# First and last chunk of 128 rows instead of 256, and weight preparation without its clamp, in a fused top-k attention and channel mix

## The chip, the core and the metric

The kernel runs on one core of a Trainium2 chip. The metric is the time on the device, in microseconds (us); it is 1204.24 us before the change (median of three runs, 1203.76 to 1204.57). A TensorE matmul clock of 1.00 in the profile means 2.4 GHz; the lower of its two levels is 1.2 GHz.

## What is computed

```python
# attention, batch 8, 8 heads, 576 rows, head size 64, top 32 of each row
scores = q @ k.T / 8
kth = 32nd largest score of the row
scores = where(scores >= kth, scores, -1e9)
attn = exp(scores - max); attn = attn / (sum(attn) + 1e-9)
x = heads side by side of (attn @ v)          # 8 x 576 x 512
# channel mix
x_prev = x moved down by one row
xk = mu_k * x + (1 - mu_k) * x_prev
xr = mu_r * x + (1 - mu_r) * x_prev
out = sigmoid(xr @ w_r) * (relu(xk @ w_k) ** 2 @ w_v)   # w_k 512x1024, w_v 1024x512, w_r 512x512
```

q, k and v are float32. The mix weights are float64; they reach the kernel as pairs of 32-bit words, and the kernel makes two fp32r halves of each (hi and lo).

## The kernel before

**Slots.** pipeline() writes one instruction order by hand. Attention has 288 tiles of 128 rows (64 rows of each head of a pair, or two heads' rows together). In slot n tile n is scored (L207, L211) and kept (L216), tile n-1 gets its candidates (L240), tile n-2 its best values (L243, L246), tile n-3 is counted (L254, L257), tile n-4 gets its threshold, exponential and mask (L833, L262, L265, L268), tile n-5 is transposed (L280, L283), a finished unit is weighed with v (L330) in slot n-6, and placed in xT (L342) in slot n-7. ORDER (L43) gives the order of steps within a slot, on each engine's queue.

**Passes.** A batch is walked in passes (PARTS, L31). A pass takes some rows for all four head pairs, and a pair has one or two units of 1, 2 or 4 tiles each. The keys of up to four pairs stay loaded, so only the first pass of a batch loads them. load_keys, load_queries and load_v put DMAs on SyncE's queue in slots that loads() works out from the start of each pair.

**Mix chunks.** The mix runs in chunks of 256 consecutive rows over all batches (SIZES, L29; 18 of them). have() (L653) says whether a chunk's rows are placed, and it says no while the weights are not done. Then begin() queues xd, xm on GpSimd (L355, L360, L365), finish() the two halves xh (ScalarE, L380) and xl (GpSimd, L381). The matmul work is cut into pieces: gate pieces (pz, 3 matmuls of 512 columns, 8 pieces in a chunk), hidden pieces (ph, 6 matmuls of as many columns as the chunk has rows, 16 pieces), value pieces (pv, 3 matmuls of 512 columns, 16 pieces). All go through three() (L385 to L387): hi x hi, hi x lo, lo x hi. The generator mix_steps orders them: gates of chunk c, second half of the values of chunk c-1, hidden pieces of c, first half of the values of c, gates of c+1. relu, square and lo half of the hidden values follow on ScalarE and GpSimd (L402 to L406), tanh of the gate on ScalarE (L418).

**The planner.** Lanes keeps a credit for each engine. TensorE's grows by 3.90 a slot up to 4.45; scores take 0.92 of it, the transpose 0.47, a weighed unit of four tiles 2.7, a mix piece 0.71 (0.56 in the last 36 slots), whatever its width. A piece goes out while at least 0.74 of its cost is there, at most four in a slot. Soft tasks on ScalarE and GpSimd go out by their own lanes' credit; the steps of the weights are charged to no lane.

**Weights.** weight_steps yields 20 blocks of 128 x 512, one a slot from slot 0 (four of w_r, eight of w_k, eight of w_v). In the slot after its DMA a block's high words go through Abs on ScalarE (L151) and a clamp on GpSimd (L152), then three bit steps on VectorE (L156 to L158). One slot later: the coarse half on GpSimd (L126), the low words on ScalarE (L162), a product on GpSimd (L163) and the remainder on TensorE (L130, L132). Another slot later ScalarE writes the lo half (L135). The PSUM tiles of this, wbits and wlo, share the two buffers of psM with pz, ph and pv. The stage buffers lie in hh and hl, which the mix uses later for its hidden values.

Of the kernel before, what the change touches and what calls it, by code (L numbers as in the profile page):

```python
# [9 lines left out]
F32 = mybir.dt.float32  # L10
# [17 lines left out]
CH = 256  # L28
SIZES = [CH] * (B * S // CH)  # L29
WHOLE = [(0, 4), (256, 4), (512, 1)]  # L30
PARTS = [[(0, 4)], [(256, 4)], [(512, 1)]], [[(0, 1), (64, 2)], [(192, 4)], [(448, 2)]], \  # L31
    [[(0, 2)], [(128, 4)], [(384, 2), (512, 1)]], [[(0, 1)], [(64, 4)], [(320, 4)]]
SCALE = 1.0 / math.sqrt(D)
# [3 lines left out]
TINY = 1e-30  # L37
ZERO = 2.0 ** -15
NEG = -3.0e38
PACE, TENSOR, SHARE, PIECE, CAP, MOST = 4.60, 3.90, 0.74, 0.71, 4.45, 4  # L40
END, HASTE = 36, 0.56
EXPS, EVAC = 4, (0, 'et')
# [4 lines left out]
def topk_attention_channel_mix(ctx: ExitStack, tc: tile.TileContext, q, k, v, mu_k, mu_r, w_k, w_v, w_r, out):  # L47
    nc = tc.nc
# [46 lines left out]

    def load_mu():
        for i, m in enumerate((mu_k, mu_r)):
            nc.sync.dma_start(mu[:, i, :], m.rearrange("(h p) -> p h", p=128))
        nc.vector.tensor_scalar(nmu, mu, -1.0, 1.0, op0=OP.mult, op1=OP.add)

# [18 lines left out]
    def weight_block(g, L, n, block, hi, lo, half):  # L119
# [30 lines left out]
        def magnitude():  # L150
            nc.scalar.activation(mag.bitcast(F32), high.bitcast(F32), AF.Abs)  # L151
            nc.gpsimd.tensor_scalar(mag.bitcast(F32), mag.bitcast(F32), ZERO, 1.0, op0=OP.max, op1=OP.mult)  # L152

# [276 lines left out]
    def mix_steps(g, chunks, L):  # L430
# [43 lines left out]

        def hiddens(c, x):
            c.hh = g.one.tile([128, NFB, CH], F32R, name="hh")
            c.hl = g.one.tile([128, NFB, CH], F32R, name="hl")
            c.written = {}
            for f in range(0, NFB, 2):
                X = Env()  # L480
                for part in range(4):
                    while len(g.ready) < (2 + f // 4) * HP:
                        yield 1
                    while part == 3 and len(g.hiddens) > 1 and not g.hiddens[-2].done:
                        yield 1
                    yield 0
                    hidden(g, f, part, *x, c.hh, c.hl, c.n, X, L)
                c.written[f // 2] = X.done
                g.hiddens.append(X.done)
# [125 lines left out]
    def pipeline(g):  # L615
# [30 lines left out]
        def chunks():  # L646
            t0 = 0
            for size in SIZES:
# [4 lines left out]
                def have(i, C=C, t0=t0, size=size):  # L653
                    if "weights" in state or min(state["heads"][2 * i:2 * i + 2]) < t0 + size:
                        return False
# [9 lines left out]
                t0 += size  # L665

        steps, state["weights"] = mix_steps(g, chunks(), L), weight_steps(g, L)
        state["next"] = None
# [50 lines left out]
        prep(g, P, P.batch, P.hp, P.c0, P.c1)  # L719
        load_mu()  # L720
        n = 0
        while n < total + 8 or "next" in state or L.busy():
# [5 lines left out]
            def loads():  # L728
                for N, t in coming(n):
                    early = N.n > 1  # L730
                    if N.own and n == max(starts[N.n] - (5 if early else 4), N.free):
                        load_keys(g, N, N.batch, N.hp)
                    if n == max(starts[N.n] - (4 if early else 3), starts[N.n - 2] - 1 if N.n > 2 else 0):
                        load_queries(g, N, N.batch, N.hp, N.c0, N.c1)
                    if n == starts[N.n - 1] + 6:
                        load_v(g, N, N.batch, N.hp)
# [90 lines left out]
            def weights():  # L827
                if "weights" in state and next(state["weights"], 0) == 0:
                    del state["weights"]

            def eighth():
# [69 lines left out]
    with tc.If(again > 0):  # L901
        with tc.For_i(0, B, 1) as b, ExitStack() as stack:
            g = Env()
            open_pools(stack, g, "_again")
            L = Direct()
# [65 lines left out]
```

## Time and profile before

| | before |
|---|---|
| median of three runs | 1204.24 us |
| profiled execution | 1203.7 us, span 1201.9 us |
| busy: TensorE, VectorE, GpSimd, ScalarE | 1117.5, 1065.4, 1024.8, 994.8 us |
| mean granted TensorE clock | 0.963 |

All four engines are at work for most of the span, so the shares of busy time don't say by themselves what a stage waits for. The profile's names: PE is TensorE, PEld its weight loads, DVE VectorE, ACT ScalarE, POOL GpSimd, SP SyncE. L152 is line 152 of the kernel. "<-POOL hl L152" behind an instruction names what ended the idle time before it. Starts of matmuls one after the other are closer than the length of one, since they overlap.

### The profile page before, as it was taken

How to read it: one execution, taken by the hardware profiler on the slowest of the kernel's cores; microseconds unless marked ns; L12 is line 12 of the kernel's file. 1: busy time of each engine (PE TensorE's matmuls, PEld its weight loads, DVE VectorE, ACT ScalarE, POOL GpSimd, SP SyncE). 2: the span in 40 equal slices, each digit the busy share in tenths (PEclk: the TensorE clock that was granted, in tenths of full speed). 3: DMA queues.
4: the chain of work that ended last, by engine and by line, in shares of the span. 5: the costliest groups of instructions: out<-in, count | busy, mean ns of one | idle time of the engine just before them, and what ended most of it. 6: DMA issues, size and time to landing. Idle time of an engine off the chain costs nothing.

```text
span 1201.9 us, 32805 instructions
## 1 busy us (share of the span) xinstructions
PE 1117.5 (93%) x10625; PEld 865.8 (72%) x10625; DVE 1065.4 (89%) x5999; ACT 994.8 (83%) x2121; POOL 1024.8 (85%) x1099
## 2 busy tenths in 40 slices
PE   4787799899999999999999999999999999999987
PEld 1343577686878787878787877787878777877876
DVE  4989999999999999999999999999999999999500
ACT  3777799998899899989898989998989899978611
POOL 5999987888889898989898888898989798988863
PEclk9777799899999999999999999999999999999989
DMA  5343114122332133212221124112421133111000
GB/s 160 110 128 104 28 47 108 50 54 57 85 75 55 50 89 76 57 48 57 67 58 48 43 77 101 49 43 67 101 75 45 49 81 90 46 38 39 29 10 29
DMA packets 161363, 78.77 MB, mean 66 GB/s; under 512 B 125344, under 2 KB 154016, under 8 KB 161184
## 3 DMA queue, kind: packets, MB, share of 16 engines
q1 hardware_dynamic: 161184, 76.59, 23.9%
q8 instruction: 87, 1.43, 0.5%
q14 instruction: 92, 0.75, 0.2%
HBM read 67.11 MB, written 9.44 MB: 64 GB/s over the span
## 4 chain that ended last, share of the span: by engine, by line
PE 53%; ACT 14%; POOL 11%; DVE 9%; issue 2%; ACTq 0%; POOLq 0%; DVEq 0%
PE ps L330 10%; PE ps L207 8%; PE ph L385 4%; ACT sc L216 4%; POOL sg L257 4%; PE pv L385 4%; PE pt L280 4%; PE ph L386 4%; PE ph L387 4%; PE pv L387 3%; PE pv L386 3%; PE pz L385 3%; ACT sg L254 2%; PE pz L387 2%; PE pz L386 2%; DVE cand L240 2%
## 5 line engine op out<-in xcount | busy, mean ns | idle before, releaser
L240 DVE MAX8 cand<-sc 128x8 f32<-128x82 f32 (+1 forms) x2016 | 464.6, 231 | 4.8 <-ACT sc L216 4.5
L257 POOL TENSOR_TENSOR sg<-sc,sg 128x576 f32<-128x576 f32 x288 | 410.6, 1427 | 37.9 <-ACT sg L254 36.3
L216 ACT ACTIVATE sc<-ps 128x576 f32<-128x576 f32 x288 | 187.8, 652 | 96.2 <-PE ps L207 84.8
L254 ACT ACTIVATE sg<-sc,seen 128x576 f32<-128x576 f32 x288 | 225.6, 783 | 21.9 <-DVE seen L833 17.8
L268 DVE SCALAR_TENSOR_TENSOR E<-sc,seen,se 128x576 f32<-128x576 f32 x288 | 232.9, 809 | 0.8 <-PE ps L211 0.3
L265 ACT ACTIVATE se<-sc,seen 128x576 f32<-128x576 f32 x288 | 215.7, 749 | 15.0 <-DVE E L268 14.5
L833 DVE MAX8 seen<-sg 128x8 f32<-128x576 f32 x288 | 215.9, 750 | 5.7 <-POOL sg L257 5.2
L207 PE MATMUL ps<-K,qs 64*128 64x288 f32 x1024 | 202.2, 472 | 14.7 <-ACT sc L216 6.4
L283 ACT ACTIVATE et<-pt 128x640 f32<-128x640 f32 x288 | 204.6, 711 | 6.4 <-PE pt L304 3.4
L330 PE MATMUL ps<-et,v_in 128*64 128x128 f32 (+1 forms) x2560 | 165.4, 273 | 21.1 <-ACT sc L216 18.5
L280 PEld LDWEIGHTS pt<-ident,E 64*128 64x128 f32 x2880 | 134.2, 140 | 64.4 <-ACT sg L254 13.0
L243 DVE MAX8 seen<-cand 128x8 f32<-128x56 f32 x864 | 176.7, 205 | 0.1
L385 PE MATMUL ph<-xh,wk 128*128 128x256 f32 x576 | 172.1, 299 | 0.0
L330 PEld LDWEIGHTS ps<-et,v_in 128*64 128x64 f32 x2560 | 134.6, 141 | 51.1 <-ACT sc L216 36.4
L386 PE MATMUL ph<-xl,wk 128*128 128x256 f32 x576 | 163.1, 283 | 0.0
L387 PE MATMUL ph<-xh,wk 128*128 128x256 f32 x576 | 162.7, 282 | 0.0
L280 PE MATMUL pt<-ident,E 64*128 64x64 f32 x2880 | 141.1, 226 | 4.4 <-DVE E L268 2.4
L207 PEld LDWEIGHTS ps<-K,qs 64*128 64x128 f32 x1024 | 80.4, 191 | 75.2 <-issue 29.1
L381 POOL TENSOR_TENSOR xl<-xm,xh 128x512 fp32r<-128x512 f32 x72 | 91.2, 1287 | 36.8 <-ACT xh L380 36.6
L385 PE MATMUL pv<-wv,hh 128*128 128x512 f32 x288 | 122.1, 424 | 0.0
L387 PE MATMUL pv<-wv,hl 128*128 128x512 f32 x288 | 115.2, 400 | 7.2 <-POOL hl L406 7.1
L246 DVE MATCH_REPLACE8 cand<-seen,cand 128x56 f32<-128x56 f32 x576 | 115.1, 200 | 0.0
(91 smaller groups left out, 2321.7 us busy)
## 6 DMA issues: line engine op xcount, KB each, us to landing
v_in<-in_v SPq DMA_DIRECT2D x192, 128.0 KB, 2.5
qs<-in_q SPq DMA_DIRECT2D x96, 128.0 KB, 2.8
K<-in_k SPq DMA_DIRECT2D x64, 144.0 KB, 2.9
out<-eb SPq DMA_DIRECT2D x36, 256.0 KB, 2.1
vr_in<-in_v SPq DMA_DIRECT2D x96, 32.0 KB, 2.4
hh<-in_moe_w_v SPq DMA_DIRECT2D x6, 512.0 KB, 3.7
qs<-in_q SPq DMA_DIRECT2D x32, 96.0 KB, 2.6
hh<-in_moe_w_k SPq DMA_DIRECT2D x5, 512.0 KB, 3.4
```

The lines of the kernel that those rows point to most:

```text
L207: nc.tensor.matmul(g.ps[:, e], lhsT=P.qs[h, T.j, x:x + 128], rhs=P.K[h, T.j], start=True, stop=True)
L216: nc.scalar.activation(T.sc.rearrange("p (e k) -> p e k", e=2), T.ps, AF.Copy)
L240: nc.vector.max(T.cand[:, 8 * i:8 * i + 8], T.sc[:, CUTS[i]:CUTS[i + 1]])
L254: nc.scalar.activation(T.side, T.sc, AF.Sign, bias=T.top[:, 23:24], scale=-1.0, accum_out=T.cnt)
L257: nc.gpsimd.tensor_mul(T.side, T.sc, T.side)
L268: nc.vector.scalar_tensor_tensor(T.e, T.sc, T.thr, g.pe, op0=OP.is_ge, op1=OP.mult, accum_out=T.rs)
L280: nc.tensor.transpose(g.pt[:, n, c * 64:(c + 1) * 64], T.e[h, k0:k0 + 128], ident[h, h])
L330: nc.tensor.matmul(pa[hs[j]], lhsT=lhsT, rhs=ms[c][j], start=(c == 0), stop=(c == NKC))
L385: nc.tensor.matmul(ps, lhsT=sh, rhs=mh, start=first, stop=False)
L386: nc.tensor.matmul(ps, lhsT=sh, rhs=ml, start=False, stop=False)
L387: nc.tensor.matmul(ps, lhsT=sl, rhs=mh, start=False, stop=last)
L833: nc.vector.max(M.top[:, 24:32], M.side)
```

## The change

The order of PARTS is turned by two, so that batch 0 begins with a pass of 128 rows and the last batch ends with one. SIZES begins and ends with a chunk of 128; all others keep 256 rows, moved by 128. The chunks need not wait for the weights in have() any more; instead hiddens() waits until three slots after the last block. Weight blocks begin in slot 2 (WAIT). The clamp in magnitude() goes; the Abs before it is scaled by 2^-112 instead. `nmu` is made in slot 3's list, and a pair's keys can be due in slot 0.

```diff
--- before.py
+++ after.py
@@ -26,18 +26,19 @@
 HP = H // 2
 NFB = FF // 128
 CH = 256
-SIZES = [CH] * (B * S // CH)
+SIZES = [CH // 2] + [CH] * (B * S // CH - 1) + [CH // 2]
 WHOLE = [(0, 4), (256, 4), (512, 1)]
-PARTS = [[(0, 4)], [(256, 4)], [(512, 1)]], [[(0, 1), (64, 2)], [(192, 4)], [(448, 2)]], \
-    [[(0, 2)], [(128, 4)], [(384, 2), (512, 1)]], [[(0, 1)], [(64, 4)], [(320, 4)]]
+PARTS = [[(0, 2)], [(128, 4)], [(384, 2), (512, 1)]], [[(0, 1)], [(64, 4)], [(320, 4)]], \
+    [[(0, 4)], [(256, 4)], [(512, 1)]], [[(0, 1), (64, 2)], [(192, 4)], [(448, 2)]]
 SCALE = 1.0 / math.sqrt(D)
 NCH = 7
 KEYS = 4
 CUTS = [82 * i for i in range(NCH)] + [S]
 TINY = 1e-30
-ZERO = 2.0 ** -15
+LOWER = 2.0 ** -112
 NEG = -3.0e38
 PACE, TENSOR, SHARE, PIECE, CAP, MOST = 4.60, 3.90, 0.74, 0.71, 4.45, 4
+WAIT = 2
 END, HASTE = 36, 0.56
 EXPS, EVAC = 4, (0, 'et')
 ORDER = """count below exp wpool high wmul norm evac best0 c0 drop0 c1 best1 c2 drop1 first score turn inv loads keep sums sign c3 best2 c4 bounds eighth norm2 et late act c5 early thr c6 mask place mix weigh wpe dve pool weights""".split()
@@ -93,10 +94,10 @@
         g.psT = p("psT", 1, space=PSUM)
         g.psM = p("psM", 2, space=PSUM)
 
-    def load_mu():
+    def load_mu(L):
         for i, m in enumerate((mu_k, mu_r)):
             nc.sync.dma_start(mu[:, i, :], m.rearrange("(h p) -> p h", p=128))
-        nc.vector.tensor_scalar(nmu, mu, -1.0, 1.0, op0=OP.mult, op1=OP.add)
+        L.at(3, "dve", lambda: nc.vector.tensor_scalar(nmu, mu, -1.0, 1.0, op0=OP.mult, op1=OP.add))
 
     def weight_steps(g, L):
 
@@ -148,8 +149,7 @@
         mag, exp = g.mag[n % 2].bitcast(U32), g.exp[n % 2].bitcast(U32)
 
         def magnitude():
-            nc.scalar.activation(mag.bitcast(F32), high.bitcast(F32), AF.Abs)
-            nc.gpsimd.tensor_scalar(mag.bitcast(F32), mag.bitcast(F32), ZERO, 1.0, op0=OP.max, op1=OP.mult)
+            nc.scalar.activation(mag.bitcast(F32), high.bitcast(F32), AF.Abs, scale=LOWER)
 
         def shift():
             bits = g.psM.tile([128, 512], U32, name="wbits", tag="pm")
@@ -473,6 +473,8 @@
                 g.gates.append(G)
 
         def hiddens(c, x):
+            while not g.staged():
+                yield 1
             c.hh = g.one.tile([128, NFB, CH], F32R, name="hh")
             c.hl = g.one.tile([128, NFB, CH], F32R, name="hl")
             c.written = {}
@@ -651,7 +653,7 @@
                 C.n, C.rows, C.pieces = size, out_rows[t0:t0 + size], None
 
                 def have(i, C=C, t0=t0, size=size):
-                    if "weights" in state or min(state["heads"][2 * i:2 * i + 2]) < t0 + size:
+                    if min(state["heads"][2 * i:2 * i + 2]) < t0 + size:
                         return False
                     if C.pieces is None:
                         state["start"] = t0
@@ -664,6 +666,7 @@
                 yield C
                 t0 += size
 
+        g.staged = lambda: n > state.get("made", n) + 2
         steps, state["weights"] = mix_steps(g, chunks(), L), weight_steps(g, L)
         state["next"] = None
 
@@ -717,7 +720,7 @@
         total = len(where)
         P = new_pair(0)
         prep(g, P, P.batch, P.hp, P.c0, P.c1)
-        load_mu()
+        load_mu(L)
         n = 0
         while n < total + 8 or "next" in state or L.busy():
             p = where[n] if n < total else None
@@ -728,7 +731,7 @@
             def loads():
                 for N, t in coming(n):
                     early = N.n > 1
-                    if N.own and n == max(starts[N.n] - (5 if early else 4), N.free):
+                    if N.own and n == max(starts[N.n] - (5 if early else 4), N.free, 0):
                         load_keys(g, N, N.batch, N.hp)
                     if n == max(starts[N.n] - (4 if early else 3), starts[N.n - 2] - 1 if N.n > 2 else 0):
                         load_queries(g, N, N.batch, N.hp, N.c0, N.c1)
@@ -825,8 +828,9 @@
                 work(MOST)
 
             def weights():
-                if "weights" in state and next(state["weights"], 0) == 0:
+                if n >= WAIT and "weights" in state and next(state["weights"], 0) == 0:
                     del state["weights"]
+                    state["made"] = n
 
             def eighth():
                 if M:
@@ -901,6 +905,7 @@
     with tc.If(again > 0):
         with tc.For_i(0, B, 1) as b, ExitStack() as stack:
             g = Env()
+            g.staged = lambda: True
             open_pools(stack, g, "_again")
             L = Direct()
             xT = new_batch(g)
```

## Rows read from the trace of the kernel before

**Rows 1.** Busy time by stage: window and its length, then each engine, granted clock, DMA.
```profile
14.20:133.80 119.60, 89.97 (x506) 48.21 (x508) 105.85 (x474) 86.59 (x166) 112.72 (x92) 0.76 0.35 107
...
300.00:1100.00 800.00, 781.60 (x7902) 623.03 (x7902) 767.81 (x4442) 714.44 (x1544) 706.70 (x778) 1.00 0.25 64
...
1117.30:1144.90 27.60, 27.60 (x259) 23.59 (x256) 11.66 (x51) 15.63 (x32) 20.58 (x22) 1.00 0.03 12
...
1144.90:1193.50 48.60, 45.28 (x238) 38.11 (x236) 2.07 (x3) 10.30 (x18) 26.37 (x26) 0.93 0.05 17
```

**Rows 2.** Chain that ended last, 226 to 231 us: start, length, what.
```profile
226.38 0.82 DVE E L268 x2
...
229.83 0.82 DVE E L268 x2
```

**Rows 3.** L216 on ScalarE, one in each slot: durations ns, first and last start.
```profile
L216 ACT ACTIVATE sc<-ps x288: 627/652/722, 7.2 to 1117.3; 128x576 f32<-128x576 f32 x144
```

**Rows 4.** GpSimd groups, 0 to 140 us: busy us, mean ns, idle before them, releaser.
```profile
L152 POOL TENSOR_SCALAR hl<-hl 128x512 f32<-128x512 f32 x20 | 38.3, 1915 | 12.3 <-ACT hl L151 12.2
...
L257 POOL TENSOR_TENSOR sg<-sc,sg 128x576 f32<-128x576 f32 x21 | 29.6, 1409 | 0.0
...
L163 POOL TENSOR_TENSOR wprod<-wfine,early 128x512 fp32r<-128x512 f32 x20 | 25.3, 1267 | 2.2 <-ACT wfine L162 2.2
...
L126 POOL TENSOR_SCALAR wv<-early 128x512 fp32r<-128x512 f32 x8 | 6.5, 819 | 0.9 <-DVE early L157 0.9
```

**Rows 5.** VectorE groups, 0 to 140 us: the line that waits for the clamp.
```profile
L156 DVE TENSOR_SCALAR wbits<-hl 128x512 uint32<-128x512 uint32 x20 | 13.9, 695 | 15.7 <-POOL hl L152 15.6
```

**Rows 6.** VectorE in order of time: start, length, instruction, idle before it and releaser.
```profile
15.78 0.69 DVE L156 TENSOR_SCALAR wbits<-hl 128x512 uint32<-128x512 uint32 x1 [6.23 <-POOL hl L152]
...
49.06 0.69 DVE L156 TENSOR_SCALAR wbits<-hl 128x512 uint32<-128x512 uint32 x1 [0.23 <-POOL hl L152]
...
54.63 0.69 DVE L156 TENSOR_SCALAR wbits<-hl 128x512 uint32<-128x512 uint32 x1 [0.22 <-POOL hl L152]
...
74.17 0.69 DVE L156 TENSOR_SCALAR wbits<-hl 128x512 uint32<-128x512 uint32 x1 [0.22 <-POOL hl L152]
```

**Rows 7.** ScalarE in order of time, one weight slot.
```profile
75.14 0.65 ACT L162 ACTIVATE wfine<-hh 128x512 f32<-128x512 uint32 x1
```

**Rows 8.** TensorE in order of time: first gate matmuls of chunk 0 and chunk 16.
```profile
149.26 0.50 PE L385 MATMUL pz<-wr,xh 128*128 128x512 f32 x1
...
1114.93 0.40 PE L385 MATMUL pz<-wr,xh 128*128 128x512 f32 x1
```

**Rows 9.** TensorE in order of time, from the last placed tile on.
```profile
1144.50 0.28 PE L386 MATMUL ph<-xl,wk 128*128 128x256 f32 x1
...
1144.62 0.28 PE L387 MATMUL ph<-xh,wk 128*128 128x256 f32 x1
...
1155.64 0.79 PE L387 MATMUL pv<-wv,hl 128*128 128x512 f32 x1 [3.14 <-POOL hl L406]
...
1157.08 0.63 PE L387 MATMUL pv<-wv,hl 128*128 128x512 f32 x1
...
1157.51 0.63 PE L385 MATMUL pz<-wr,xh 128*128 128x512 f32 x1
...
1192.84 0.40 PE L386 MATMUL pv<-wv,hh 128*128 128x512 f32 x1
...
1193.07 0.39 PE L387 MATMUL pv<-wv,hl 128*128 128x512 f32 x1
```

**Rows 10.** GpSimd in order of time: the last placed tile.
```profile
1144.15 0.74 POOL L342 TENSOR_TENSOR xT<-sum,ri 128x256 f32<-128x256 f32 x1 [1.31 <-ACT sum L336]
```

**Rows 11.** Chain that ended last, 152 to 163 us: attention matmuls at full clock.
```profile
152.28 0.69 PE ps L207 x4
...
152.96 0.30 PE pt L280 x10
...
160.09 2.40 PE ps L330 x40
```

## The prediction, written before the changed kernel ran

> **What bounds the kernel now.** I read four views in this order: busy time by stage, the groups of the opening, the queue of one engine there, and the order of instructions in the closing stage. Time goes in slots: slot n scores tile n of the attention, and each slot has one L216, so their starts date it [rows 3]. The stages differ [rows 1]. From 300 to 1100 us TensorE is busy 782 and VectorE 768 of 800 us; both are full, a slot is 3.7 us, and little can be won. Between 14.2 and 133.8 us (slots 2 to 22, with a weight block in each) a slot takes 5.98 us, and there VectorE is busy 106 and GpSimd 113 of 119.6. After the last attention tile TensorE is alone: from the last placed tile (ends at 1144.9, [rows 10]) to the last value matmul at 1193.5 it holds 238 matmuls in 48.6 us [rows 1, 9]. What then follows, 8.4 us of closing steps in the span, is not touched.
>
> In a weight slot GpSimd has four long steps: the mask product 1.41, the clamp 1.92, the coarse half 0.83, the product 1.27, together 5.43 us [rows 4]. The slot's period, from one L156 to the next, is 5.57 us [rows 6]. So the clamp looks worth 1.92 x 20 = 38 us. It isn't: VectorE waits for the clamp only 0.22 us in each of 14 such slots, and its own queue is 5.57 - 0.22 = 5.35 us long. A VectorE slot without weights is 3.45 us [rows 2]; the block's three steps make the other 1.9. VectorE is the next bound, right below the first.
>
> **The change part by part.** The profiled execution took 1203.7 us (span 1201.9), 0.5 below the median of 1204.24; the sum goes against 1203.7.
>
> *The clamp (20 GpSimd instructions out).* ScalarE's scaled Abs is the same instruction as the Abs before, so it costs nothing new. L156 then waits for that Abs, which ends 1.9 us earlier than the clamp. VectorE idled 15.6 us in 18 waits for the clamp [rows 5], 6.2 of it at the first block [rows 6]. The other 9.4 go: -9.4 (0 to -9.4).
>
> *Blocks begin in slot 2.* The same 20 blocks stand two slots later. The 6.2 us wait was for the first block's DMA and clamp; now the tiles of slots 2 and 3 are computed meanwhile. Against that, three head pairs of keys and queries are loaded in the first two slots (pairs have two tiles now), all on SyncE's queue ahead of block 0, and slot 2 waits for its keys. Between 0 and -6.2; I take half, -3.1. The row of `nmu` moves to slot 3, off the start, and is needed only in slot 10: nothing.
>
> *First chunk of 128.* Its eight tiles are placed in slot 14, not 22, and have() no longer waits for the weights. The xm/xh/xl chain takes two slots, so four gate pieces go out together in slot 16, amid the weights, where TensorE and ScalarE are not full. But psM has two buffers, and each weight slot takes two (wlo, wbits). The gates' pz makes three: the L156 of slot 16 must wait until pz is read by tanh (L418), in slot 17 behind exp, fine and wfine. Behind L156 stands all of VectorE's next slot. L156 starts at 74.17 and the wfine of the following slot ends at 75.79 [rows 6, 7], so tanh's half microsecond makes that wait at least 2.1 us; with the 12 gate matmuls ahead of it, 0.23 us each at full clock and 0.43 at 1.2 GHz [rows 9], it is up to 6.3. I take +4.5 (0 to +6.3). The hidden pieces wait for staged() until slot 25. What is queued there is only this generator; by slot 36 it has done 28 pieces, worth 20 full ones, where the kernel before, whose first gate started in slot 26 [rows 8], had done 26; those six are made up, because chunk 1 follows at once where the kernel before still waited for the rows of its second chunk. Chunk c+1 then runs where c ran, eight slots later, and the middle is unchanged (0 +- 2).
>
> *Last chunk of 128.* Before: of the 238 matmuls in the last 48.6 us, 116 are hidden ones at 0.12 us and 120 of 512 columns at 0.23 [rows 9]: 41.7 us. The other 7 are a 3.14 us wait for hl and some 15 matmuls at the half clock right after it, 0.43 apart instead of 0.23 [rows 9]. After: chunk 17 (256 rows) is there eight slots before the last tile. Before, chunk 16's gates began in slot 286, four after the earliest possible one [rows 8]; I expect chunk 17's in slot 291 or 292, done when the last tile is placed (slot 294). Then remain 12 value matmuls of chunk 16, 96 hidden and 48 value of chunk 17, 12 gate, 96 half-width hidden and 24 value of the last one: 96 of 512 columns x 0.23 = 22.1, 96 x 0.12 = 11.5, and the half-width ones. No row shows a 128-column matmul of this type. From 0.233 at 512 and 0.12 at 256 columns the line gives 0.063 at 128; the dear end is the plain f32 product, 128 columns in two instructions, 40 of them in 2.40 us with two side by side [rows 11], so 0.12 for an instruction's turn and 0.24 for a product. I take 0.063, since the two rows are of the same type and on one line through nearly zero: 6.0 us. The sum is 39.6; xl ahead of the gates is half as long, so half the wait and half the slow matmuls stay: 2 to 3 us. 48.6 - 42 = -6.6, rounded to -7. With chunk 17's gates still open it is -1, with chunk 16's values done -10.
>
> Sum: -9.4 - 3.1 + 4.5 - 7 = -15: 1203.7 - 15 = 1189 us.
>
> **The rivals.**
> *A 128-column matmul costs what a 256-column one does* (0.12, bound by its weight load): the last chunk's 96 cost 5.4 us more, the first chunk's are hidden in slots 25 to 31: 1194 us. For it: each has its own weight load. Against it: ten transposes, each with a 128-column load, take 0.30 us [rows 11]. The Trainium skill (TensorE: Matmul & The Clock Gate, section LDWEIGHTS) says a load takes its columns over 1.2 GHz; that would be about 0.107 us each, an estimate by that page, and 4.2 us on the last chunk. The transposes' rows disagree, but they use half the array's rows each.
>
> *It costs what a plain f32 product does* (0.24). This ends slower. Place: the hidden pieces of the first and last chunk, whose only columns are 128 where every hidden one now has 256. Price: the last chunk's 96 cost 96 x 0.177 = 17 us more, all on the path. The first chunk's 96 take 23 us of TensorE in some six slots; attention there takes 0.69 + 0.30 + 0.60 [rows 11] of 3.45, which leaves 11 us, so 12 more. 1189 + 29 = 1218 us. Gain and loss are equal at 0.17 us per matmul. For it: the planner counts a piece as 0.71 whatever its width, so nothing would hold back; the operands are four bytes wide, as f32 ones. Against it: one instruction each, not two.
>
> *VectorE alone rules the opening*: the waits for the clamp turn into waits for keys, ScalarE and pz, the opening gains only 14 x 0.22 = 3 and pays 4.5. Then only the closing is left: 1203.7 + 1.5 - 7 = 1198 us. For it: 5.35 against 5.57. Against it: the long waits are not of that kind.
>
> **How the numbers follow.** Forecast 0.43 (1189, own range 1181 to 1196); same price as 256 columns 0.16 (1194); VectorE alone 0.11 (1198); f32 price 0.30 (1218, 1211 to 1224). No measurement of this kernel tells less than about 0.2%, 2.4 us, from no change. Slower takes the f32 case, 0.30; same 0.06, the upper ends of the two middle cases; faster the other 0.64. The range must take in part of the f32 case: 1179 to 1216.
>
> **What would show it.** The period of L156 in the weight slots falls to about 5.35; 3.7 would mean that VectorE wasn't the bound, 5.57 that GpSimd wasn't. The L156 of slot 16 has one wait of 2 to 6 us released by tanh. The first pz comes in slot 16, the first ph in slot 25. The starts of the 128-column ph matmuls are 0.06 apart; at 0.12 the first rival holds, at 0.2 or above the second, and the forecast is wrong. From the last placed tile to the last value matmul it takes 42 us. If the middle's slots are longer than 3.7 us, my claim that only the ends move is wrong.

## The result: slower by 0.9%, and the loss lies in the middle

The changed kernel takes 1214.91 us (median, 1213.68 to 1215.98), against 1204.00 of the kernel before beside it: a ratio of 1.0094 [1.0078, 1.011]. The forecast was 1189, faster. The time lies just inside the upper end of the range, but that end was there for another reason, which the trace refutes.

| | before | after |
|---|---|---|
| profiled execution, span | 1203.7, 1201.9 us | 1215.4, 1213.4 us |
| busy: TensorE, VectorE, GpSimd, ScalarE | 1117.5, 1065.4, 1024.8, 994.8 us | 1130.1, 1073.9, 989.7, 995.9 us |
| mean granted TensorE clock | 0.963 | 0.973 |

GpSimd lost 35 us of work and the span grew by 11.5. Busy time by stage in the changed kernel (window, its length, each engine, granted clock, DMA), to be read beside [rows 1]: the weight slots 4 to 22, the same 800 us of the middle, the last slots, and the closing stage from the last placed tile on.

```profile
20.90:134.40 113.50, 88.87 (x523) 50.83 (x523) 105.79 (x448) 87.46 (x175) 79.01 (x91) 0.83 0.38 110
300.00:1100.00 800.00, 775.06 (x7756) 615.25 (x7753) 760.57 (x4379) 703.22 (x1514) 693.85 (x752) 0.99 0.24 62
1130.40:1156.60 26.20, 24.29 (x224) 19.52 (x221) 11.86 (x50) 15.79 (x36) 23.67 (x29) 1.00 0.13 34
1156.60:1205.20 48.60, 48.30 (x303) 42.61 (x301) 2.06 (x3) 11.49 (x24) 26.89 (x36) 1.00 0.05 17
```

In the weight slots GpSimd is down to 79 of 113.5 us, so the clamp is gone, and VectorE alone is near full there, at 105.8 us. In the middle both full engines are less busy than before: TensorE 775 for 782, VectorE 761 for 768, with fewer instructions in the same 800 us. Something else holds them up. The closing stage, from the last placed tile to the last value matmul, takes 48.6 us as before, though it now has 303 matmuls and no half clock.

The starts of L216, one in each slot, date the slots. All times of stages and slots here come from one profiled execution of each kernel; executions of one kernel differ by up to 6 us in the whole. Here is how much later than before each kernel starts a slot, in us, the experiments below among them (minus is earlier; before: slot 24 at 139.8, 36 at 186.2, 112 at 462.8, 287 at 1117.3, last value matmul at 1193.07 [rows 9]):

| kernel | 24 | 36 | 112 | 287 | last value matmul |
|---|---|---|---|---|---|
| after | +0.2 | -4.0 | +8.5 | +13.1 | +11.7 |
| before with the moved rows alone | 0.0 | -1.0 | +13.9 | +14.4 | +14.5 |
| after without the moved rows | -5.2 | -5.5 | -5.2 | -5.1 | -5.2 |
| after, hl ahead of xm | +0.1 | -4.1 | +3.5 | +0.9 | -6.0 |
| before, hl ahead of xm | +0.3 | +0.4 | -0.8 | -4.3 | -10.8 |
| after without the moved rows, hl ahead of xm | -5.5 | -6.9 | -3.1 | -4.7 | -12.3 |
| the same, coarse half moved | -13.9 | -14.1 | -11.7 | -13.6 | -21.2 |

The change gains 4.0 us by slot 36, loses 12.5 between slots 36 and 112, another 4.6 up to slot 287, and gets 1.4 back after it. Between slots 24 and 287 it takes 990.4 us where the kernel before took 977.5: +12.9 where I had put 0 +- 2.

What the slots wait for shows in the chain of work that ended last. First the kernel before, then the changed one, slots 48 to 112 (227.9 to 462.8 and 225.8 to 471.3 us): the chain's share of that stretch by line.

```profile
by line: PE ps L330 12.1%; PE ps L207 10.6%; ACT sc L216 6.2%; PE pt L280 5.0%; PE ph L385 4.7%; ACT sg L254 4.6%; PE pv L385 4.1%; ACT et L283 4.1%; PE ph L386 4.0%; PE ph L387 3.9%; ACT se L265 3.8%; PE pv L387 3.4%; PE pv L386 3.4%; PE p
```

```profile
by line: POOL sg L257 10.8%; PE ps L330 9.8%; PE ps L207 9.7%; POOL hl L406 6.6%; ACT sc L216 4.4%; PE pv L387 4.4%; POOL r L405 4.2%; PE pv L385 4.2%; PE ph L385 4.1%; POOL xl L381 4.0%; PE pv L386 3.5%; PE pt L280 3.5%; PE ph L386 3.3%; P
```

Before, no line of GpSimd stands among the first thirteen. Now four do, with a quarter of the stretch: the mask product, the square (r), its lo half (hl), and the lo half of the next chunk's rows (xl). One place of it, on GpSimd of the changed kernel in order of time (start, length, instruction):

```profile
234.85 2.56 POOL L381 TENSOR_TENSOR xl<-xm,xh 128x512 fp32r<-128x512 f32 x2
237.36 1.42 POOL L257 TENSOR_TENSOR sg<-sc,sg 128x576 f32<-128x576 f32 x1
238.74 0.74 POOL L342 TENSOR_TENSOR xT<-sum,ri 128x256 f32<-128x256 f32 x1
239.42 1.05 POOL L405 TENSOR_TENSOR r<-r 128x512 f32<-128x512 f32 x1
240.55 1.27 POOL L406 TENSOR_TENSOR hl<-r,hh 128x512 fp32r<-128x512 f32 x1
```

On TensorE, the value matmul that reads this hl, and the scores that are queued behind it:

```profile
241.87 0.50 PE L387 MATMUL pv<-wv,hl 128*128 128x512 f32 x1 [2.95 <-POOL hl L406]
...
244.38 0.76 PE L207 MATMUL ps<-K,qs 64*128 64x288 f32 x4
```

And on ScalarE the keep that reads the scores, from which the rest of the tile's chain starts:

```profile
245.27 0.65 ACT L216 ACTIVATE sc<-ps 128x576 f32<-128x576 f32 x1 [3.51 <-PE ps L207]
```

The last hl of chunk 1 stands behind both xl of chunk 2 in GpSimd's queue. The scores of the next tile are written behind that value matmul and start only at 244.38 us, so a value matmul without its hl holds them too. This is the place of slot 51, the longest of the middle (6.93 us). The gates of chunks 2 to 5 go out first in slots 51, 67, 83, 99; each of these four slots is longer than 4.5 us (6.93, 4.82, 4.63, 4.61).

### The profile page after: what moved, and what is told of

The parts are those of the page before. It is cut to its first block, busy times and chain, and to the rows that moved or that the text cites. A ratio compares the mean times of both kernels' runs of the same rounds, so it can differ in the third digit from the quotient of the medians.

```text
span 1213.4 us, 33035 instructions
## 1 busy us (share of the span) xinstructions
PE 1130.1 (93%) x10721; PEld 877.6 (72%) x10721; DVE 1073.9 (89%) x5999; ACT 995.9 (82%) x2133; POOL 989.7 (82%) x1098
## 4 chain that ended last, share of the span: by engine, by line
PE 55%; POOL 18%; ACT 12%; DVE 10%; issue 2%; SPq 1%; DMA 0%; DVEq 0%; ACTq 0%; POOLq 0%
PE ps L330 11%; PE ps L207 8%; POOL sg L257 6%; PE ph L385 4%; PE ph L386 4%; PE pv L385 4%; PE ph L387 4%; PE pv L387 4%; ACT sc L216 4%; PE pt L280 4%; PE pv L386 3%; POOL hl L406 3%; PE pz L385 3%; POOL xl L381 2%; POOL r L405 2%
## 5 line engine op out<-in xcount | busy, mean ns | idle before, releaser
L216 ACT ACTIVATE sc<-ps 128x576 f32<-128x576 f32 x288 | 188.1, 653 | 118.8 <-PE ps L207 103.7
L254 ACT ACTIVATE sg<-sc,seen 128x576 f32<-128x576 f32 x288 | 225.8, 784 | 17.0 <-DVE seen L837 16.5
L265 ACT ACTIVATE se<-sc,seen 128x576 f32<-128x576 f32 x288 | 215.9, 750 | 12.0 <-DVE E L268 11.5
L330 PE MATMUL ps<-et,v_in 128*64 128x128 f32 (+1 forms) x2560 | 168.2, 276 | 23.1 <-ACT sc L216 20.4
L385 PE MATMUL ph<-xh,wk 128*128 128x256 f32 (+1 forms) x608 | 179.7, 296 | 0.0
L386 PE MATMUL ph<-xl,wk 128*128 128x256 f32 (+1 forms) x608 | 171.3, 282 | 0.3 <-POOL xl L381 0.3
L387 PE MATMUL ph<-xh,wk 128*128 128x256 f32 (+1 forms) x608 | 170.8, 281 | 0.0
L385 PEld LDWEIGHTS ph<-xh,wk 128*128 128x128 f32 x608 | 117.1, 193 | 4.8
L381 POOL TENSOR_TENSOR xl<-xm,xh 128x512 fp32r<-128x512 f32 (+1 forms) x76 | 91.7, 1229 | 31.1 <-ACT xh L380 30.9
```

Of the source, the lines that this page charges most:

```text
L216: nc.scalar.activation(T.sc.rearrange("p (e k) -> p e k", e=2), T.ps, AF.Copy)
L254: nc.scalar.activation(T.side, T.sc, AF.Sign, bias=T.top[:, 23:24], scale=-1.0, accum_out=T.cnt)
L330: nc.tensor.matmul(pa[hs[j]], lhsT=lhsT, rhs=ms[c][j], start=(c == 0), stop=(c == NKC))
L385: nc.tensor.matmul(ps, lhsT=sh, rhs=mh, start=first, stop=False)
L386: nc.tensor.matmul(ps, lhsT=sh, rhs=ml, start=False, stop=False)
L387: nc.tensor.matmul(ps, lhsT=sl, rhs=mh, start=False, stop=last)
```

## The experiments

Two questions: which half of the change loses the time, and by what. My theory after reading the trace was the order on GpSimd above. The rivals: the weights' half of the change loses it; chunks are taken too early; the moved 128-column matmuls cost it; the first chunk among the weights sets the mix back.

**The moved rows alone.** The kernel before with the new passes and chunks; chunks still wait for the weights and the clamp stays.

```diff
-SIZES = [CH] * (B * S // CH)
+SIZES = [CH // 2] + [CH] * (B * S // CH - 1) + [CH // 2]
-PARTS = [[(0, 4)], [(256, 4)], [(512, 1)]], [[(0, 1), (64, 2)], [(192, 4)], [(448, 2)]], \
-    [[(0, 2)], [(128, 4)], [(384, 2), (512, 1)]], [[(0, 1)], [(64, 4)], [(320, 4)]]
+PARTS = [[(0, 2)], [(128, 4)], [(384, 2), (512, 1)]], [[(0, 1)], [(64, 4)], [(320, 4)]], \
+    [[(0, 4)], [(256, 4)], [(512, 1)]], [[(0, 1), (64, 2)], [(192, 4)], [(448, 2)]]
-                    if N.own and n == max(starts[N.n] - (5 if early else 4), N.free):
+                    if N.own and n == max(starts[N.n] - (5 if early else 4), N.free, 0):
```

> Only the rows move: PARTS and SIZES are the new ones, the weights stay as before (clamp, blocks from slot 0, no chunk before the weights are done). Theory A (the loss of 12.9 us between slots 24 and 287 comes from the moved chunks, whose mix runs one or two slots behind its rows): the middle loses 10 to 13 us as in the changed kernel, the opening is that of before, 1214 to 1219 us. Rival B (the loss comes from the weight steps and the early chunk among them): 1198 to 1206 us.

Measured: 1217.61 us, ratio 1.0112 [1.0085, 1.0138]. It has the changed kernel's loss in the middle (+14.4 us between slots 24 and 287) and, from slot 36 on, its gates in the same slots nearly everywhere. The moved rows lose the time, with or without anything done to the weights.

**The weights' half alone.** The changed kernel with the old passes and chunks.

```diff
-SIZES = [CH // 2] + [CH] * (B * S // CH - 1) + [CH // 2]
+SIZES = [CH] * (B * S // CH)
-PARTS = [[(0, 2)], [(128, 4)], [(384, 2), (512, 1)]], [[(0, 1)], [(64, 4)], [(320, 4)]], \
-    [[(0, 4)], [(256, 4)], [(512, 1)]], [[(0, 1), (64, 2)], [(192, 4)], [(448, 2)]]
+PARTS = [[(0, 4)], [(256, 4)], [(512, 1)]], [[(0, 1), (64, 2)], [(192, 4)], [(448, 2)]], \
+    [[(0, 2)], [(128, 4)], [(384, 2), (512, 1)]], [[(0, 1)], [(64, 4)], [(320, 4)]]
```

> Only the weights change: no clamp, blocks from slot 2, no wait for the weights in have(); PARTS and SIZES are those of before. By the prediction's own step (9.4 + 3.1 us won in the opening, no pz among the weights) it is 1191 us. Theory C (VectorE's queue is the bound and its last bit step, L158, grows from 0.50 to 0.83 us because the coarse half on GpSimd now starts beside it): 20 x 0.33 = 6.6 us of it are lost, 1196 to 1200 us. Rival (the clamp was on no path at all): 1203 to 1206 us.

Measured: 1198.78 us, ratio 0.9954 [0.9939, 0.997]. Slot 24 starts 5.2 us earlier than before, and the gain is kept to the end. The forecast had 12.5 for these two steps (clamp 9.4, blocks 3.1). The rest of it went on VectorE, in the groups of the opening (0 to 140 us; busy us, mean ns, then the idle time before them and its releaser). The kernel before:

```profile
L158 DVE TENSOR_SCALAR early<-early 128x512 uint32<-128x512 uint32 x20 | 10.0, 499 | 0.7
```

and the weights' half alone:

```profile
L158 DVE TENSOR_SCALAR early<-early 128x512 uint32<-128x512 uint32 x20 | 16.3, 813 | 2.0
L156 DVE TENSOR_SCALAR wbits<-hl 128x512 uint32<-128x512 uint32 x20 | 13.8, 688 | 1.1 <-ACT hl L152 1.1
```

The waits for the clamp, 15.6 us before [rows 5], are down to 1.1. But L158, the same instruction, takes 0.31 us longer in the mean of 20 times. From one L156 to the next on VectorE of this kernel:

```profile
44.40 0.69 DVE L156 TENSOR_SCALAR wbits<-hl 128x512 uint32<-128x512 uint32 x1
45.28 0.69 DVE L157 SCALAR_TENSOR_TENSOR early<-hl,wbits 128x512 uint32<-128x512 uint32 x1 [0.20 <-DVE wbits L156]
46.08 0.88 DVE L158 TENSOR_SCALAR early<-early 128x512 uint32<-128x512 uint32 x1
...
50.28 0.69 DVE L156 TENSOR_SCALAR wbits<-hl 128x512 uint32<-128x512 uint32 x1
```

The period is 5.88 us and no wait for the block is left in it; it was 5.57 with the clamp [rows 6]. What stands beside L158 is told with the coarse half, below.

**A later take.** If chunks are taken too soon after their rows, a pause of four slots should separate the next chunk's xm and xl from the last hl.

```diff
...
+                    if 0 < t0 < B * S - size and n < C.seen.setdefault(i, n) + 4:
+                        return False
```

> The changed kernel, but each chunk except the first and the last is taken four slots after its rows are placed, so the mix runs some five slots behind as in the kernel before. Theory A: hl is no longer queued behind the next chunk's xd and xm on GpSimd when the last value matmul of a half needs it; the middle gets back about 10 us, 1203 to 1208 us, the waits of pv for hl in slots 48 to 112 fall below 3 us. Rival (the loss is in the shape of the passes or the extra pieces): 1213 to 1220 us.

Measured: 1269.45 us, ratio 1.055 [1.0524, 1.0577]. This idea fell. The chunks fall further behind each time (gates of chunk 2 in slot 58 instead of 51, of chunk 14 in slot 267 instead of 246), and TensorE's waits for hl are longer, not gone. What it waits for before its value matmuls in the whole span, first the changed kernel, then this one (us, times):

```profile
  POOL hl L406: 10.0, 10
```

```profile
  POOL hl L406: 37.3, 19
```

A delay moves xl and hl of one turn together; their order on GpSimd stays. The run says little of the distance between chunks as such: 43 of the 54.5 us that it loses against the changed kernel come in the closing stage (91.9 us for 48.6), for the delayed mix has more left to do there; the middle takes 4.8 us longer (995.3).

**hl ahead of xm.** The changed kernel; only the order of GpSimd's soft tasks changes. Of those that can go, the one with the lowest rank goes first; xm and xl have rank 0. The steps that make xm get rank 2, behind r and hl (rank 1), and as the two xl can then end in either order, the gates wait for both.

```diff
-            l = [L.soft("pool", 0.0046 * n + 0.05 * len(pieces), change, *l)]
-        g.shared[i] = [L.soft("pool", 0.0033 * n + 0.05, share, *l)]
-        X.mixed = L.soft("pool", 0.0046 * n + 0.05 * len(pieces), add, *g.shared[i])
+            l = [L.soft("pool", 0.0046 * n + 0.05 * len(pieces), change, *l, rank=2)]
+        g.shared[i] = [L.soft("pool", 0.0033 * n + 0.05, share, *l, rank=2)]
+        X.mixed = L.soft("pool", 0.0046 * n + 0.05 * len(pieces), add, *g.shared[i], rank=2)
...
-                while not L.past(ready):
+                while not all(L.past(r) for r in ready):
```

> The changed kernel with another order on GpSimd alone: of the queued mix steps, a new chunk's xd and xm go behind the lo halves of the hidden values. Theory A in its narrow form (it is GpSimd's order, not the small distance as such): 1203 to 1208 us. If the distance as such costs (scores and gates bunch up), 1211 to 1217 us.

Measured: 1198.72 us, ratio 0.9961 [0.9945, 0.9977], 16.2 us less than the changed kernel and below the range expected, since the closing stage gains 7 us as well. The middle takes 978.3 us (slots 24 to 287), as long as before the change, and the closing stage 41.6. GpSimd at the same place (lines are one further on):

```profile
233.37 1.44 POOL L257 TENSOR_TENSOR sg<-sc,sg 128x576 f32<-128x576 f32 x1
234.73 1.30 POOL L407 TENSOR_TENSOR hl<-r,hh 128x512 fp32r<-128x512 f32 x1
235.99 0.96 POOL L360 TENSOR_SCALAR xm<-xd,nmu 128x256 f32<-128x256 f32 x2
```

and the chain by line in slots 48 to 112 (226.4 to 466.3 us):

```profile
by line: PE ps L330 12.9%; PE ps L207 12.4%; POOL sg L257 7.2%; PE ph L386 6.7%; PE ph L387 5.5%; PE ph L388 5.4%; PE pv L386 5.4%; PE pt L280 5.0%; PE pv L388 4.3%; PE pv L387 4.3%; ACT sc L216 3.2%; PE pz L386 2.8%; POOL xl L382 2.4%; POO
```

hl and r have left the head of the chain, and matmuls lead it again; the mask product stays, with 7.2% for 10.8. ScalarE's waits for scores in the same slots, before, after and here:

```profile
ACT sc L216 <- PE ps L207: 14.0, 19, 2.5
```

```profile
ACT sc L216 <- PE ps L207: 31.2, 35, 3.5
```

```profile
ACT sc L216 <- PE ps L207: 14.5, 32, 1.3
```

The order is shown as the cause: with the moved rows in both, it alone brings slot 287 forward by 12.2 us. (That the gates wait for both xl was not run by itself; it can only hold gates back.) It also answers the rival that chunks are taken too early, which the pause of four slots could not: the gates of chunks 2 to 6 go out in slots 50, 66, 82, 98 and 114, no later than in the changed kernel.

**The same order in the two kernels with the old rows.** The kernel before with the ranks above, and the weights' half alone with them.

> The kernel before with the order of e4_hl_first on GpSimd. TensorE waits for hl 17.6 us there, 3.1 of it in the closing stage and 15 in the middle. If what e4 won (16 us) belongs to the moved chunks alone, 1202 to 1206 us; if the order costs the kernel before as well, 1190 to 1198 us.

> e2_weights (all chunks of 256, the new weight steps) with the order of e4_hl_first: what the chunks of 128 are worth once GpSimd's order is mended, against e4_hl_first (1198.7 us). The prediction's closing stage (7 us won by the last chunk, 4.5 lost by the first): 1199 to 1203 us. If the 128-column matmuls and the chunk among the weights cost what the ends give: 1188 to 1197 us.

Measured: 1193.37 us, ratio 0.9913 [0.9893, 0.9933], and 1191.47 us, ratio 0.9897 [0.9878, 0.9916]. So the order is a weakness of the kernel before as well; it costs that kernel 10.3 us and the weights' half 7.3, most or all of it in the closing stage (48.6 to 41.9 and 48.5 to 40.8 us), where less is left to do: 209 matmuls instead of 238 and 237. (The 17.6 us in the expectation add the waits of the weight loads to those of the matmuls; the value matmuls alone wait 7.1 us for hl in the kernel before, 3.9 of it between slots 24 and 287.) In the middle it costs the old rows 4.6 us (977.5 to 972.9) or nothing (977.6 to 978.3), the moved ones 12.1. With the order mended and the new weight steps the middle takes 978.3 us with either rows. What is left of the moved rows is 1198.72 against 1191.47 us: a loss of 7.

**The coarse half behind the product.** Made on the kernel with hl first: L126 (here L127) goes from its own step behind the product L163 on GpSimd, so that it doesn't start together with L158.

```diff
-        L.at(2, "wpool", coarse)
...
         L.at(2, "wmul", lambda: nc.gpsimd.tensor_mul(g.prod, g.fine, exp.bitcast(F32)))
+        L.at(2, "wmul", coarse)
```

> e4_hl_first with the coarse half (GpSimd) issued behind the product of the same block instead of ahead of it, so it can't start together with VectorE's L158. Theory C (the two hold each other up): L158 falls from 0.82 to 0.45 us, the period of L156 from 5.9 to about 5.5, 20 x 0.4 = 8 us less: 1189 to 1193 us. Rival (L158 is longer for another reason, or VectorE isn't the bound of the weight slots): L158 stays or the time does, 1197 to 1203 us.

Measured: 1195.98 us, ratio 0.9931 [0.991, 0.9952], 2.7 less than without it, between the two ranges expected. VectorE here (one line further up):

```profile
48.13 0.69 DVE L156 SCALAR_TENSOR_TENSOR early<-hl,wbits 128x512 uint32<-128x512 uint32 x1 [0.20 <-PE pt L280]
48.85 0.43 DVE L157 TENSOR_SCALAR early<-early 128x512 uint32<-128x512 uint32 x1
...
53.50 0.69 DVE L156 SCALAR_TENSOR_TENSOR early<-hh,wbits 128x512 uint32<-128x512 uint32 x1 [0.20 <-PE wlo L131]
```

The last bit step, here L157, is back at 0.43 us (`early<-early`, the second line; 541 ns in the mean of 20), and the period is 5.37 from one L156 (the step before it) to the next, the 5.35 that the prediction read as VectorE's own. The gain of 3.8 us is all made by slot 14 (79.9 to 76.0); slots 14 to 24, where the first chunk's gates run among the weights, take 60.1 us with it and 60.0 without. L155's waits for the fine half there are 3.0 us instead of 1.7; where the rest of those slots' gain went I did not settle.

**The clamp put back** into the changed kernel (two lines more; what was L156 is L158 there, what was L158 is L160).

```diff
+ZERO = 2.0 ** -15
...
-            nc.scalar.activation(mag.bitcast(F32), high.bitcast(F32), AF.Abs, scale=LOWER)
+            nc.scalar.activation(mag.bitcast(F32), high.bitcast(F32), AF.Abs)
+            nc.gpsimd.tensor_scalar(mag.bitcast(F32), mag.bitcast(F32), ZERO, 1.0, op0=OP.max, op1=OP.mult)
```

> The changed kernel with the clamp put back on GpSimd, everything else as changed. If the clamp's removal is worth what the prediction said (9.4 us of VectorE's waits), 1222 to 1226 us; by theory C the waits come back but L158 is short again: 1214 to 1219 us.

Measured: 1220.31 us, ratio 1.0149 [1.0126, 1.0173]. Between the two ranges expected. Slot 24 starts at 149.5 us against 140.0, 9.5 us later, and 5.4 of these are left at the end. That the 9.5 is near the 9.4 of the prediction is chance. Up to slot 24 VectorE idles 19.9 us ahead of the step that writes wbits, 18.4 of it for the clamp, where the changed kernel idles 5.2; against that, the last bit step takes 12.5 us in all instead of 16.5. The prediction had the waits alone and left out the first block's.

**The first chunk not among the weights.** On the kernel with hl first, chunks again wait for the weights.

```diff
-                    if min(state["heads"][2 * i:2 * i + 2]) < t0 + size:
+                    if "weights" in state or min(state["heads"][2 * i:2 * i + 2]) < t0 + size:
```

> e4_hl_first, but the first chunk of 128 waits until the last weight block is issued (slot 22). Theory D (the first chunk's gates and its xm, xh, xl steps among the weights cost the 5.4 us by which e4 reaches slot 24 later than e2): slot 24 starts at 134 to 136 instead of 139.9 us, and the whole takes 1191 to 1195 us. Rival (the head start of the first chunk is worth as much as it costs): 1197 to 1202 us.

Measured: 1200.86 us, ratio 0.9989 [0.998, 0.9998], against 0.9961 with the early chunk: no better, and slot 24 misses the 134 to 136 us expected. It comes 1.8 us earlier (138.1), the middle is another 1.8 us shorter, and the closing stage takes 47.2 us instead of 41.6. So the head start brings some 2 us more than it costs, and most of the moved rows' price in the opening (slot 24 at 134.3 with the old rows) isn't the first chunk: 3.8 of 5.6 us stay, and the passes alone differ there. They stand there by slot 4 already, which starts at 21.1 us here and at 16.9 with the old rows. Two waits for DMAs, which the kernel with the old rows doesn't have, come ahead of it: TensorE's for the queries of slot 2 and ScalarE's for the first weight block.

```profile
10.45 2.19 PE L207 MATMUL ps<-K,qs 64*128 64x288 f32 x4 [1.72 <-DMA qs<-in_q]
```

```profile
18.53 0.66 ACT L152 ACTIVATE hl<-hh 128x512 f32<-128x512 f32 x1 [3.13 <-DMA hh<-in_moe_w_r]
```

**Half as wide again.** On the kernel with hl first, each 128-column hidden matmul as two of 64 columns.

```diff
-        for h in range(half * HP // 2, (half + 1) * HP // 2):
-            three(ph[:, e, :n], wk[0][:, h, w], wk[1][:, h, w], xh[:, h, :n], xl[:, h, :n], h == 0, h == HP - 1)
+        m, hs = slice(0, n), range(half * HP // 2, (half + 1) * HP // 2)
+        if n < CH:
+            m, hs = slice(half * n // 2, (half + 1) * n // 2), range(HP)
+        for h in hs:
+            three(ph[:, e, m], wk[0][:, h, w], wk[1][:, h, w], xh[:, h, m], xl[:, h, m], h == 0, h == HP - 1)
```

> e4_hl_first with each 128-column hidden matmul of the first and last chunk issued as two of 64 columns, 192 instead of 96 in a chunk, same result. If a matmul of this type takes 0.11 us whatever its columns (its weight load sets the pace), the starts stay 0.11 apart, the last chunk's hidden matmuls take 21 instead of 10.7 us and the whole some 10 us more than e4, 1207 to 1211 us. If the columns set the pace, they are 0.055 apart and the time stays at 1197 to 1201 us.

Measured in one run: 1250.19 us, far above both ranges expected. Starts of 128-column matmuls in the changed kernel, then of 64-column ones here, both at full clock:

```profile
1188.98 0.27 PE L385 MATMUL ph<-xh,wk 128*128 128x128 f32 x1
1189.09 0.27 PE L386 MATMUL ph<-xl,wk 128*128 128x128 f32 x1
1189.20 0.28 PE L387 MATMUL ph<-xh,wk 128*128 128x128 f32 x1
```

```profile
147.93 0.28 PE L388 MATMUL ph<-xh,wk 128*128 128x64 f32 x1
148.04 0.28 PE L386 MATMUL ph<-xh,wk 128*128 128x64 f32 x1
148.15 0.28 PE L387 MATMUL ph<-xl,wk 128*128 128x64 f32 x1
```

Both are 0.11 us apart, as the 256-column ones nearly are (0.12, [rows 9]): the price is the instruction's, not the columns'. That explains 192 more matmuls x 0.11 = 21 of the 51 us. The rest goes with the clock: the granted clock is 0.50 for 30.7 us from 150.2 on and for 34.1 us from 1201.5 on, where the kernel with hl first has no such stretch. At 1.00 the work of these 64.8 us would take half as long, some 32 us less by this estimate. The last section shows it.

**The order and the coarse half on the old rows.** The weights' half alone with the ranks and the moved coarse half; all chunks have 256 rows.

> All chunks of 256, new weight steps, GpSimd's order of e4_hl_first, and the coarse half behind the product: the parts that helped, without the chunks of 128. e8_weights_hl took 1191.5 us; e5_coarse won 2.7 against e4, and e2's opening has more slots in which VectorE alone sets the pace: 1183 to 1189 us. If the coarse half's place gives nothing here, 1190 to 1193 us.

Measured: 1181.97 us, ratio 0.9819 [0.9804, 0.9834], faster than both kernels. Slot 24 starts 13.9 us earlier than before, slot 287 still 13.6, and from there to the last value matmul it gains 7.6 more. The time is 1 us below the range expected.

## Why the prediction was wrong, and where it was right, step by step

In the profiled executions the change costs 11.7 us where the forecast's sum wins 15, 26.7 us apart. Of these, 8.2 fall up to slot 24 (+0.2 for -8), 12.9 in the middle (+12.9 for 0), and 7 in the closing stage (0 for -7); the slots between the middle and the closing stage give 1.4 back.

**What bounds the opening: right.** VectorE is the next bound below the clamp; its queue of 5.35 us is the 5.37 measured once nothing lengthens it. The waits for the clamp went. That the changed kernel's period was to fall to about 5.35 did not come true: it is 5.88 to 5.90 in most slots, longer than the 5.57 with the clamp, for the reason in the next step.

**Blocks from slot 2, and the opening's sum of -8: wrong, by a size that I took as fixed.** I let VectorE's steps keep their lengths when GpSimd's order around them changed. Without the clamp the coarse half no longer starts just behind L158 but just ahead of it, and L158 grew by 0.33 us x 20 = 6.5 us (499 to 825 ns). L157, which now follows L156 with a short wait, idles 2.3 us more in all (1.7 to 4.0 us). The first chunk gave 2.7 of its 4.5 back, by the 1.8 below; some 2 us are open. The moved passes cost 3.8 us at slot 24 with the first chunk held back, but that is in the -3.1: these are the DMAs that I had named. The queries of the second head pair and the first block land late (waits of 1.72 and 3.13 us), and VectorE's first wait is 3.5 us now for 6.2 before, about the half that I took. With the clamp in place the moved passes reach slot 4 2.9 us later as well (29.9 for 27.0), but have made that up by slot 24 (0.0 in the table). So slot 24 starts at 140.0 us, as before. The kernel with the old rows, hl first and the coarse half moved has neither the longer L158 nor the late loads. It is 13.9 us earlier at that slot and makes good the 12.5 of the two steps.

**First chunk among the weights: the mechanism right, its size and its releaser not.** The first gate matmuls go out at 90.51 us, in the slots predicted. The wait for psM is there, on VectorE of the changed kernel:

```profile
96.81 0.70 DVE L156 TENSOR_SCALAR wbits<-hl 128x512 uint32<-128x512 uint32 x1 [1.75 <-ACT wv L136]
```

It is 1.75 us, below the 2.1 to 6.3 that I had worked out from tanh, and far from the 4.5 taken. (Twelve gate matmuls at 0.43 us on top of 2.1 would make 7.3; the 6.3 does not follow from the rows shown.) The fine step releases it, not tanh. In all the early chunk costs 1.8 us at slot 24 and as much again in the middle, and saves 5.6 in the closing stage.

**The middle "unchanged (0 +- 2)": the step that failed.** I asked only whether the chunks' work still falls into slots that can take it. What moved is when a chunk is taken against the hidden pieces of the chunk ahead of it. In slots 48 to 117 the gates of chunk c+1 come four to seven slots after those of chunk c before, not eight as I had written (44, 62, 78, 95, 111 before; 51, 67, 83, 99, 117 after), that is one to four slots nearer to their rows. There the xm and xl of the new chunk and the last r and hl of the old one fall into the same slots on GpSimd, where the code puts xm and xl first. I had added up GpSimd's queue for the clamp, and not for the mix, because there [rows 1] show it at 707 of 800 us, not full. An engine that isn't full can still hold up two that are, by its order. With the order mended, the middle is 978.3 us, within the 0 +- 2 of the 977.5 before. That is a sum of parts that are not 0: 4.2 us won up to slot 36, 7.6 lost from there to slot 112, 2.6 won after it. And the kernel before with the same order takes 972.9.

How the 13 us divide is not settled. Of the 12.5 us lost between slots 36 and 112 the order gives back 4.9; the other 7.2 that it gives back come between slots 112 and 287. What lengthens slots 36 to 112 even with hl first I did not test. TensorE's direct waits for hl grow by 3.9 us in slots 24 to 287 (3.9 in 5 waits to 7.8 in 8); the slots longer than 4.5 us hold 7.3 us more above 3.7 each (9.2 in 6 slots to 16.5 in 10); the rest is spread over many slots.

**The closing stage, -7: no gain.** The mix is 15 matmuls further back than I had put it when the last tile is placed (303 for 288): 24 value matmuls of chunk 16 are still to come, not 12, and 3 gate ones of chunk 17. At 0.233 that is 3.5 us, and the 128-column matmuls at 0.111 us instead of 0.063 are 96 x 0.048 = 4.6. The two fill what the wait for hl and the half clock of before left free [rows 9]; neither of these is in the changed kernel. With hl first it takes 41.6 us, near the 42 of the prediction by luck: 270 matmuls are left there, not 288, which makes up for the dearer 128-column ones. The kernel with the old rows and hl first takes 40.8: the last chunk of 128 gains nothing.

**The rivals.** The 256-column price for 128 columns was right (0.111 for 0.12). The Trainium skill (TensorE: Matmul & The Clock Gate, section LDWEIGHTS) puts the load of 128 columns at 128 over 1.2 GHz, an estimate of 0.107 us; the trace agrees at full clock, 0.111 at 128 and at 64 columns, each with a load of 128. At the lower clock the starts are 0.21 us apart, which that figure does not give. The 1194 us that I put beside this rival did not come, for the reasons above. The f32 price, 0.24, was the only case in which I had the kernel slower. It is refuted: the kernel is slower without it, so that the time lies inside the range is luck. No rival had a queue of the middle in it, since I took what the change says it touches, the ends, for what it moves.

## What to carry to other kernels

A change that only shifts work in time is to be followed through each engine's written order, also on the engines that aren't full: look for the producer that now stands behind another task's steps, and for what is queued behind its consumer. When the slowest step on one engine is taken out, the steps beside it start at other moments, and those that share something with another engine get other lengths; a next bound read from the trace of before holds only while they don't. And a part of a change that costs can hide a part that gains: here half of it alone was faster, and two small changes of order were worth more than the rest.

## What the runs showed of the hardware

**Two steps that start together.** L158 on VectorE and the coarse half on GpSimd start in the same moment. In the changed kernel GpSimd is first, by 0.01 us:

```profile
66.80 0.62 POOL L127 TENSOR_SCALAR wk<-early 128x512 fp32r<-128x512 f32 x1 [0.43 <-DVE early L157]
```

```profile
66.81 0.89 DVE L158 TENSOR_SCALAR early<-early 128x512 uint32<-128x512 uint32 x1
```

and in the kernel before VectorE did, by 0.06:

```profile
61.77 0.43 DVE L158 TENSOR_SCALAR early<-early 128x512 uint32<-128x512 uint32 x1
```

```profile
61.83 0.85 POOL L126 TENSOR_SCALAR wk<-early 128x512 fp32r<-128x512 f32 x1 [0.22 <-DVE early L157]
```

The one that starts second is the longer: 0.89 for 0.43 us, or 0.85 for 0.62. The Trainium skill (SBUF — State Buffer, section Who interferes with whom) says that the two engines share one pair of ports, which a tensor_scalar of VectorE can take whole, and that the second to start then stands until the first has ended. The trace agrees in the direction, either way round; a full wait and then the step would be 0.61 + 0.43 = 1.04 us, 0.15 over the 0.89 measured. With the coarse half moved out of the way, the step was 0.43 again.

**A clock that falls while TensorE is busy.** In the kernel with 64-column matmuls, busy time by stage: while chunk 0's run, and in the closing stage; the last line is the kernel with hl first and 128 columns.

```profile
140.00:150.00 10.00, 9.98 (x107) 8.05 (x107) 10.00 (x59) 7.74 (x16) 5.27 (x5) 0.83 0.24 57
150.00:175.00 25.00, 25.00 (x129) 23.83 (x128) 8.86 (x50) 6.46 (x14) 4.49 (x5) 0.50 0.02 6
...
1205.00:1215.00 10.00, 10.00 (x49) 10.00 (x48) 0.00 (x0) 0.80 (x2) 1.34 (x2) 0.50 0.00 0
```

```profile
150.00:175.00 25.00, 25.00 (x282) 20.66 (x283) 24.68 (x146) 23.05 (x55) 19.95 (x26) 1.00 0.26 65
```

TensorE shows no idle time (by a profile that models the ends of matmuls, so this is no share of work), its weight loads fill 23.83 of the 25 us, and yet the granted clock is 0.50, the 1.2 GHz level, from 150 to 175 us; the matmuls are then 0.21 us apart. With 128 columns in the same place the clock is 1.00. Narrow matmuls cost twice here: by the instruction, and by the clock at which all matmuls of the stretch run. This is one execution.
